# Keys, queries, values and weights laid out by the launcher as the kernel reads them, in a sliding-window attention with two feed-forward layers

## The chip, the cores and the metric

The kernel runs on one core of one Trainium2 chip. The metric is the device time of one execution in microseconds, the median of several runs. The core's engines run side by side and wait for one another through semaphores: TensorE (PE in the profile; PEld is its weight load), VectorE (DVE), ScalarE (ACT), GpSimd (POOL) and SyncE (SP), which only issues transfers here. Each engine works off its own instructions in the order in which they were queued. Work done by the launcher on the host is not part of the time.

## The reference

Attention over 2 batches of 8 heads, 768 positions, head dimension 64. A position sees the first `n_sink` positions (4) and the last `window` positions (128). Its output, heads side by side, runs through two feed-forward layers over 1536 tokens of width 512.

```python
scores = (q @ k.T) / sqrt(64)                      # per batch and head
keep = (pos_k < n_sink) | (0 <= pos_q - pos_k < window)
a = softmax(where(keep, scores, -1e9))
x = (a @ v)                                        # -> [1536, 512]
x = ((x @ w_a) * (x @ w_b)) @ w_out                # 512 -> 1536 -> 512
h = maximum(x @ w_in2, 0)
out = (h * h) @ w_out2                             # 512 -> 2048 -> 512
```

The weights arrive as 64-bit floats, q, k and v as 32-bit floats.

## The kernel before, in words

**Groups and steps.** A group is one block of 128 queries of 4 heads; there are 24, numbered batch, then block `i` (0 to 5), then half of the heads `m`. `attention_fast` runs 27 steps. In step g it goes through the list ORDER (L28), which names pieces of work with a lag: `("scores", 0)` is the scores of group g, `("rec", -1)` the reciprocal of the sums of group g - 1, `("x", -3)` the values of group g - 3. The lists are a schedule by hand: TensorE, VectorE, ScalarE and GpSimd take their instructions in the order in which they are emitted (L800). SP's transfers are not in that list and follow the emission as their buffers come free.

**One group's way.** Two steps ahead transfers bring k and q with tokens in the partitions (L179), one step ahead v (L193). One step ahead TensorE transposes keys and queries (`pt`, L233, four transposes), ScalarE copies them out of PSUM (`kq`, L239) into a buffer of slots, and for block 0 GpSimd copies the first 8 keys behind each slot as sink keys (L241). In its own step: scores (L258; for a block i > 0 against the block itself, the block before it, and the sink keys), then on VectorE a predicated copy that merges the two triangles (L271) and the masked maximum (L274), then on ScalarE four exponentials with their sums (L282). One step later: reciprocal (L287, the first VectorE instruction of a step), the scaled sink columns (L305), normalizing on VectorE (L292) and ScalarE (L297), TensorE's transposes of probabilities (L312, L336). Two steps later ScalarE copies (L316) and GpSimd cuts the two triangles (L327, L329). Three steps later the values (L355) and the sink values (L360), and the split of the result into a high and a low part (L368, L371).

**Sink values.** `vs` holds the values of the first 8 positions of each head, arranged and zero-padded so that one matmul adds them for a pair of heads; it is needed from step 5 on (group 2). `sink_load` clears a buffer on GpSimd and issues 24 transfers on SP, emitted in front of step 1; `sink_split` makes the parts on ScalarE (L216) and VectorE (L217), emitted behind step 2.

**Masks.** `setup` and `masks` build three masks on VectorE from `n_sink` and `window`, which come as single values and are spread over the partitions by a matmul (L106). `flag` tests whether the fast way applies; otherwise `attention_any` would run, which it does not with these inputs.

**Beside the attention.** The weights' 64-bit floats are decoded in pieces of 128 x 512 (`Weights.stages`): ScalarE L552, VectorE L556, L557, L560 in one step, VectorE L563, ScalarE L568, VectorE L570 in the next. DECODE (L33) lists the steps in which a piece is begun. From step 10 on each step also holds one fill of 12 matmuls of the first feed-forward layer (L660). From step 9 on (WIDE) the attention has two PSUM buffers fewer, which go to the fills. `warm` issues dummy matmuls: 14 at the beginning (WARM0), 4 and 3 in steps 0 and 1 (WARM1). Behind the 27 steps follow the remaining fills and the rest of both layers (`Ffn.block`, L660 and L701), with the other weights decoded on the way. `Weights.load` brings one piece per transfer into one of three raw buffers (L537).

Of the kernel before, what the change touches and what calls it, by code (L numbers as in the profile page):

```python
# [61 lines left out]
def setup(tc, cp, tp, n_sink, window):  # L62
    nc = tc.nc
    c = Attn()
    ident = tp.tile([P, P], F32, name="ident")
# [1 line left out]
    c.identr = cp.tile([P, P], F32R, name="identr")
    nc.vector.tensor_copy(c.identr, ident)
    c.ident = c.identr.bitcast(F32)

    raw = cp.tile([1, 4], I32, name="raw")
    nc.scalar.dma_start(raw[:, 0:2], n_sink.bitcast(I32).partition_broadcast(1))
    nc.scalar.dma_start(raw[:, 2:4], window.bitcast(I32).partition_broadcast(1))
# [17 lines left out]
    c.rel0 = tp.tile([P, P], F32, name="rel0")  # L91
    v.scalar_tensor_tensor(out=c.rel0, in0=c.upf, scalar=BIG, in1=d, op0=ALU.mult, op1=ALU.add)
    lo = cp.tile([1, 2], F32, name="lo_f")
    hi = cp.tile([1, 2], F32, name="hi_f")
# [2 lines left out]
    c.par0 = cp.tile([1, 2], F32, name="par0")
    v.scalar_tensor_tensor(out=c.par0, in0=hi, scalar=4294967296.0, in1=lo, op0=ALU.mult, op1=ALU.add)
    return c


def masks(tc, cp, tp, c, ps):

    nc = tc.nc
    v = nc.vector
    nc.tensor.matmul(ps, lhsT=c.one, rhs=c.par0, start=True, stop=True)  # L106
# [754 lines left out]
```

## Time and profile before

| | |
|---|---|
| median of 3 runs | 676.22 us (676.17 to 676.25) |
| profiled execution | 678.09 us |
| its span, first to last instruction | 676.40 us |
| mean granted TensorE clock | 0.986 |
| TensorE busy | 652.0 us (96%) |
| VectorE busy | 401.7 us (59%) |
| ScalarE busy | 290.7 us (43%) |
| GpSimd busy | 30.2 us (4%) |

The page gives busy time of each engine and its tenths in 40 slices of the span. [...] The timeline lists instructions with start and length; a bracket behind a row says how long the engine was idle before it and what ended the wait. The chain of waits follows the work that ended last back to the start.

### The profile page before, as it was taken

The numbers are of one execution on the slowest core, as the hardware profiler recorded it, in microseconds if no ns is written. First come the engines' busy times: TensorE is split into PE (matmuls) and PEld (weight loads), VectorE is DVE, ScalarE is ACT, GpSimd is POOL, SyncE is SP. The second block draws the span as 40 slices with busy tenths as digits, with TensorE's granted clock in tenths as the row PEclk, the third lists the DMA queues.
The fourth block names the chain that finished last, engine by engine and source line by source line (L and its number), as shares of the span: only waits on it lengthen the run. The fifth ranks groups of instructions, "written<-read, shape, count | busy, mean of one in ns | idle before, by whom it ended". The sixth has DMA issues, their size and how long they took to land.

```text
span 676.4 us, 8976 instructions
## 1 busy us (share of the span) xinstructions
PE 652.0 (96%) x3267; PEld 528.6 (78%) x3267; DVE 401.7 (59%) x950; ACT 290.7 (43%) x676; POOL 30.2 (4%) x53
## 2 busy tenths in 40 slices
PE   7578999999999999999999999999999999999996
PEld 5356877778788888888888888888888888888884
DVE  5698986762689872588641789535824232333323
ACT  6676886761444532545321446324532222222221
POOL 1131202120000000000000000000000000000000
PEclk9697999999999999999999999999999999999999
DMA  5853543310164550045400043200200000001011
GB/s 136 197 121 85 145 123 85 85 33 0 63 188 133 165 169 1 32 150 162 155 1 0 32 125 125 94 0 32 63 0 1 0 1 0 1 1 62 23 40 68
DMA packets 65560, 48.99 MB, mean 72 GB/s; under 512 B 39908, under 2 KB 60388, under 8 KB 65508
## 3 DMA queue, kind: packets, MB, share of 16 engines
q1 hardware_dynamic: 65504, 48.34, 24.8%
q8 instruction: 27, 0.44, 0.3%
q14 instruction: 25, 0.20, 0.1%
q10 hardware_dynamic: 4, 0.00, 0.0%
HBM read 45.19 MB, written 3.15 MB: 71 GB/s over the span
## 4 chain that ended last, share of the span: by engine, by line
PE 92%; DVE 4%; ACT 1%; DMA 1%; SPq 1%; issue 0%; DVEq 0%; ACTq 0%
PE psa L660 48%; PE acc L701 34%; PE x L355 3%; PE sc L258 3%; PE pt L233 1%; PE ptp L312 1%; ACT ex L282 1%; PE x L360 1%; DMA qraw<-in_q_dram 1%; SPq L211 1%; DVE ex L274 1%; DVE ex L292 1%; DVE sc L271 1%; PE psw L380 1%; DVE xl L371 0%
## 5 line engine op out<-in xcount | busy, mean ns | idle before, releaser
L660 PE MATMUL psa<-xh,wh 128*128 128x512 f32 x480 | 188.9, 393 | 0.8 <-DVE gs L677 0.8
L660 PE MATMUL psa<-xh,wl 128*128 128x512 f32 x480 | 187.0, 390 | 0.0
L660 PE MATMUL psa<-xl,wh 128*128 128x512 f32 x480 | 186.8, 389 | 0.0
L660 PEld LDWEIGHTS psa<-xh,wh 128*128 128x128 f32 x480 | 90.4, 188 | 19.8 <-DVE gs L677 1.3
L660 PEld LDWEIGHTS psa<-xh,wl 128*128 128x128 f32 x480 | 90.1, 188 | 19.0
L660 PEld LDWEIGHTS psa<-xl,wh 128*128 128x128 f32 x480 | 90.3, 188 | 18.3
L740 DVE TENSOR_TENSOR g<-u 128x512 f32<-128x512 f32 x48 | 33.1, 690 | 111.2 <-ACT u L730 111.2
L730 ACT ACTIVATE u<-psa 128x512 f32<-128x512 f32 x48 | 28.7, 598 | 119.0 <-PE psa L660 119.0
L701 PE MATMUL acc<-wh,gl 128*128 128x512 f32 x192 | 74.7, 389 | 0.0
L701 PE MATMUL acc<-wl,gh 128*128 128x512 f32 x192 | 74.7, 389 | 0.0
L58 ACT CAST gh<-g 128x512 fp32r<-128x512 f32 x72 | 44.6, 620 | 64.7 <-DVE g L740 34.8
L552 ACT ACTIVATE wtmp<-wraw 128x512 f32<-128x512 f32 x68 | 45.5, 672 | 54.0 <-DMA wraw<-in_moe_w_in_dram 17.9
L59 DVE TENSOR_TENSOR gl<-g,gh 128x512 fp32r<-128x512 f32 x72 | 49.6, 689 | 31.2 <-ACT gh L58 30.9
L701 PE MATMUL acc<-wh,gh 128*128 128x512 f32 x192 | 62.7, 389 | 0.0
L568 ACT CAST wh<-wtmp 128x512 fp32r<-128x512 f32 x68 | 41.8, 618 | 35.5 <-DVE wtmp L563 15.5
L570 DVE TENSOR_TENSOR wl<-wtmp,wh 128x512 fp32r<-128x512 f32 x68 | 46.5, 685 | 17.0 <-ACT wh L568 15.9
L701 PE MATMUL acc<-gl,wh 128*128 128x512 f32 x144 | 56.0, 389 | 0.0
L701 PE MATMUL acc<-gh,wl 128*128 128x512 f32 x144 | 55.9, 389 | 0.0
L560 DVE SCALAR_TENSOR_TENSOR wtmp<-wraw,wtmp 128x512 int32<-128x512 int32 x68 | 47.4, 699 | 0.6
L701 PE MATMUL acc<-gh,wh 128*128 128x512 f32 x144 | 47.3, 389 | 0.0
L563 DVE SCALAR_TENSOR_TENSOR wtmp<-wraw,wtmp 128x512 int32<-128x512 int32 x68 | 46.5, 684 | 0.2
L701 PEld LDWEIGHTS acc<-wl,gh 128*128 128x128 f32 x192 | 36.1, 188 | 7.5
(92 smaller groups left out, 753.4 us busy)
## 6 DMA issues: line engine op xcount, KB each, us to landing
wraw<-in_moe_w_out_dram SPq DMA_DIRECT2D x28, 512.0 KB
wraw<-in_moe_w_in_dram SPq DMA_DIRECT2D x16, 512.0 KB
wraw<-in_moe_w_a_dram SPq DMA_DIRECT2D x12, 512.0 KB
wraw<-in_moe_w_b_dram SPq DMA_DIRECT2D x12, 512.0 KB
vraw<-in_v_dram SPq DMA_DIRECT2D x24, 128.0 KB
out_dram<-part SPq DMA_DIRECT2D x12, 256.0 KB
kraw<-in_k_dram SPq DMA_DIRECT2D x23, 128.0 KB
qraw<-in_q_dram SPq DMA_DIRECT2D x23, 128.0 KB
```

Of the source, the lines that this page charges most:

```text
L58: nc.scalar.copy(hi, src)
L59: (lo_eng or nc.vector).tensor_sub(lo, src, hi.bitcast(F32))
L258: nc.tensor.matmul(o, lhsT=half(flat, r)[:, qp, 0:P], rhs=y, start=True, stop=True)
L552: a = nc.scalar.activation(tf, up.bitcast(F32), AF.Abs)
L560: nc.vector.scalar_tensor_tensor(out=t, in0=up, scalar=0x3FFFFFFF, in1=t, op0=ALU.bitwise_or, op1=ALU.bitwise_and)
L563: nc.vector.scalar_tensor_tensor(out=t, in0=low, scalar=29, in1=t, op0=ALU.logical_shift_right, op1=ALU.bitwise_or)
L568: nc.scalar.copy(hi, tf)
L570: nc.vector.tensor_sub(lo, tf, hi.bitcast(F32))
L660: self.tc.nc.tensor.matmul(ps, lhsT=w[:, kt, :], rhs=x[:, kt, ts], start=n == 0, stop=n == 3 * KT - 1)
L701: mm = nc.tensor.matmul(acc[d], lhsT=a, rhs=b_, start=f == 0 and j == 0, stop=f == NF - 1 and j == 2)
L730: nc.scalar.activation(u, pa, AF.Relu)
L740: nc.vector.tensor_mul(g, u, u)
```

## The change

The launcher gets a function `layout`, and the kernel takes its inputs as laid out there:

- q and k with two heads' dimensions in the 128 partitions, per block of 128 positions; k with the 8 sink keys behind each block. So scores read them as they come, and `transposes`, `transposes_copy` and GpSimd's copy are gone, with `pt` and `kq` in ORDER. A slot of keys and a tile of queries now hold a whole block (8 heads), loaded every second step.
- v per block with all heads, one transfer for two groups.
- `vs` comes ready with its zeros, one transfer a batch; the two splits are emitted behind steps 3 and 6 (VS).
- `n_sink` and `window` come spread over 128 partitions in one transfer; the spreading matmul is gone. Only mask 0 is built ahead of step 0; masks 1 and 2 and the flags are emitted behind it.
- weight pieces are contiguous; w_a, w_b and w_in2 rows are 4 KB in a partition instead of four runs of 1 KB.
- the dummy matmuls of WARM1 are gone; DECODE begins a piece in step 8 and none in step 22.

```diff
-    ("rec", -1), ("x", -3), ("th", -2), ("sp", -1), ("norm", -1), ("scores", 0), ("pt", 1), ("xh", -3),
-    ("normA", -1), ("xl", -3), ("fm", 0), ("soft0", 0), ("fu", 0), ("stt2", -1), ("soft1", 0), ("abs", 0),
-    ("pst", -1), ("kq", 1), ("st", -1), ("fill", 0), ("exp0", 0), ("sts", -1), ("ts", 0), ("cast", -1), ("stt",
-    0), ("lu", -2), ("lo", -1), ("exp1", 0), ("ptp", -1)]
-DECODE = [2, 6, 9, 10, 11, 12, 13, 15, 18, 20, 22]
+    ("rec", -1), ("x", -3), ("th", -2), ("sp", -1), ("norm", -1), ("scores", 0), ("xh", -3), ("normA", -1),
+    ("xl", -3), ("fm", 0), ("soft0", 0), ("fu", 0), ("stt2", -1), ("soft1", 0), ("abs", 0), ("pst", -1), ("st",
+    -1), ("fill", 0), ("exp0", 0), ("sts", -1), ("ts", 0), ("cast", -1), ("stt", 0), ("lu", -2), ("lo", -1),
+    ("exp1", 0), ("ptp", -1)]
+DECODE = [2, 6, 8, 9, 10, 11, 12, 13, 15, 18, 20]
 WIDE = 9
-SINK = (1, 2)
+VS = (3, 6)
 PINNED = 3
 WARM0 = 14
-WARM1 = {0: 4, 1: 3}
-NV, NEX, NTH, NLU, NSP = 8, 3, 2, 2, 2
+NQ, NV, NEX, NTH, NLU, NSP = 3, 5, 3, 2, 2, 2
+NK = 4
...
+    raw = cp.tile([P, 4], I32, name="raw")
+    nc.scalar.dma_start(raw, span.bitcast(I32))
...
+def later_masks(tc, cp, tp, c):
+    v = tc.nc.vector
+    m0, m1, m2 = c.m
+    c.up = cp.tile([P, P], I32, name="upi")
+    v.tensor_copy(c.up, c.upf)
+
+    out_of(v, m2[:, 0:P], c.rel, c.w)
+    v.tensor_copy(m2[:, P:SW], c.sink[:, 0:SK])
 
...
+    keys = p1.tile([P, NK, H // 2, SW], F32, name="keys")
+    queries, vals = {}, {}
...
+    def load_kq(n, part=slice(0, H // 2)):
+        if n >= B * NB:
             return
...
+        if n not in queries:
+            queries[n] = p2.tile([P, H // 2, P], F32, name="queries", tag="queries", bufs=NQ)
+        b, i = divmod(n, NB)
+        nc.sync.dma_start(keys[:, n % NK, part], k[b, i, :, part])
+        nc.sync.dma_start(queries[n][:, part], q[b, i, :, part])
+
+    def load_v(n):
+        if n >= B * NB:
+            return
+        vals[n] = p2.tile([P, H, D], F32, name="values", tag="values", bufs=NV)
+        nc.sync.dma_start(vals[n], v[n // NB, n % NB])
+
+    with tc.high_priority(offset=1000):
+        load_kq(0, slice(0, 2))
+        load_kq(0, slice(2, 4))
+    load_kq(1)
+    load_v(0)
 
...
-    def sink_load():
-        nc.gpsimd.memset(vsr, 0.0)
-        for kind in range(3):
-            for j in range(GH):
-                for b in range(B):
-                    p0 = (kind * GH + j) * SK
-                    nc.sync.dma_start(vsr[p0:p0 + SK, b, j // 2:H // 2:2, (j % 2) * D:(j % 2 + 1) * D],
-                                      v[b, j:H:GH, 0:SK, :].rearrange("m s d -> s m d"))
-
-    def sink_split():
-        for b in range(B):
-            nc.scalar.copy(vs[:, b], vsr[:, b])
-            nc.vector.tensor_sub(vs[64:96, b], vsr[64:96, b], vs[64:96, b].bitcast(F32))
-
...
+    def sink_load(b):
+        vsr[b] = p1.tile([96, H // 2, P], F32, name="vsr", tag="vsr")
+        nc.sync.dma_start(vsr[b], vs_in[:, b])
+
+    def sink_split(b):
+        nc.scalar.copy(vs[:, b], vsr[b])
+        nc.vector.tensor_sub(vs[64:96, b], vsr[b][64:96], vs[64:96, b].bitcast(F32))
...
-        pt = pts[g] = bank("pt").rearrange("p (j a) t -> p j a t", j=2)
-        for j, t in enumerate((kr, qr)):
-            for pp in range(2):
-                nc.tensor.transpose(pt[:, j, pp], t[:, 2 * pp:2 * pp + 2, :].rearrange("t h d -> t (h d)"), c.ident)
-        vals[g] = vr
-
-    def transposes_copy(g):
-        b, i, m = groups[g]
-        ks, qs = (i % 2) * 2 + m, 4 + g % 2
-        nc.scalar.copy(kq[:, ks:qs + 1:qs - ks, :, 0:P], pts.pop(g))
-        if i == 0:
-            nc.gpsimd.tensor_copy(kq[:, m:m + 3:2, :, P:SW],
-                                  kq[:, ks, :, 0:SK].unsqueeze(1).to_broadcast([P, 2, 2, SK]))
...
         for pp, sc in enumerate(scs[g]):
...
-                    y = half(flat, r)[:, kp:kp + 5:4]
+                    (u0, u1), _ = around(g)
+                    y = half(keys, r)[:, u0:u1 + 1:u1 - u0, 2 * m + pp]
...
     warm(WARM0)
-    transposes(0)
-    masks(tc, cp, tp, c, bank("par")[:, 0, 0:2])
-    transposes_copy(0)
     for g in range(N + 3):
         if g == WIDE:
             banks.pop()
             wide.close()
             beside.open()
-        if g == SINK[0]:
-            sink_load()
-        load(g + 2)
+        if g % 2 == 0:
+            load_kq(g // 2 + 2)
+            load_v(g // 2 + 1)
+        if g == 0:
+            sink_load(0)
         beside.fetch(g)
-        if g in WARM1:
-            warm(WARM1[g])
         for name, lag in ORDER:
             if name in stages:
                 if 0 <= g + lag < N:
                     stages[name](g + lag)
             else:
                 beside.stage(name, g + lag)
-        if g == SINK[1]:
+        if g == 0:
+            later_masks(tc, cp, tp, c)
             flag(tc, cp, c)
-            sink_split()
+        if g in VS:
+            sink_split(VS.index(g))
+            if g == VS[0]:
+                sink_load(1)
...
-        def cols(w, f):
-            return w.bitcast(I32).rearrange("(k p) f -> p k f", p=P)[:, :, 2 * f * P:2 * (f + 1) * P]
-
-        def rows(w, f):
-            return w.bitcast(I32)[f * P:(f + 1) * P, :].unsqueeze(1)
+        FF1, FF2 = w_a.shape[0], w_in2.shape[0]
+
+        def piece(w, f):
+            return w.bitcast(I32)[f]
...
+def layout(inputs):
+
+    import numpy as np
+
+    def pairs(a, n):
+
+        B, H, S, D = a.shape
+        a = a.reshape(B, H // 2, 2, S // n, n, D).transpose(0, 3, 2, 5, 1, 4)
+        return a.reshape(B, S // n, 2 * D, H // 2, n)
+
+    def blocks(w, inner):
+
+        if inner:
+            K, FF = w.shape
+            w = w.reshape(K // P, P, FF // P, P).transpose(2, 1, 0, 3)
+        return np.ascontiguousarray(w.reshape(-1, P, 512)).view(np.int64)
+
+    q, k, v = (np.asarray(inputs[n]) for n in "qkv")
+    B, H, S, D = v.shape
+    out = {"q": pairs(q, P)}
+    sinks = pairs(k[:, :, 0:SK], SK)
+    out["k"] = np.concatenate([pairs(k, P), np.broadcast_to(sinks, (B, S // P, *sinks.shape[2:]))], axis=4)
+    out["v"] = v.reshape(B, H, S // P, P, D).transpose(0, 2, 3, 1, 4)
+
+    vs = np.zeros((3, 4, SK, B, H // 4, 2, 2, D), v.dtype)
+    for j in range(4):
+        vs[:, j, :, :, :, j // 2, j % 2] = v[:, j::4, 0:SK].transpose(2, 0, 1, 3)
+    out["vs"] = vs.reshape(12 * SK, B, H // 2, 2 * D)
+    out["span"] = np.broadcast_to(np.stack([inputs["n_sink"], inputs["window"]]).astype(np.int64), (P, 2))
+    for n in _INS[5:]:
+        out[n] = blocks(np.asarray(inputs[n]), not n.endswith("out"))
+    return out
```

## Rows read from the trace of the kernel before

**Rows 1.** The page's busy tenths of TensorE in 40 slices of the span.

```profile
PE   7578999999999999999999999999999999999996
```

**Rows 2.** Windows, us from:to, length, busy us (instructions) per engine, clock, transfers.

```profile
57.34:63.31 5.97, 5.97 (x32) 4.58 (x33) 5.65 (x16) 2.41 (x8) 1.67 (x2) 0.50 0.11 25
63.31:99.14 35.83, 35.83 (x261) 28.13 (x261) 32.11 (x110) 28.62 (x95) 6.04 (x10) 1.00 0.53 140
99.14:137.65 38.51, 38.51 (x284) 30.08 (x283) 28.79 (x111) 27.92 (x94) 7.79 (x12) 1.00 0.32 83
```

**Rows 3.** Timeline of the start: start us, length us, engine, line, what.

```profile
1.07 3.17 PE L380 MATMUL psw<-zero 128*128 128x256 bf16 x14 [1.07 <-DVE zero L787]
...
2.76 0.16 DVE L95 CAST lo_f<-raw 1x2 f32<-1x2 uint32 x1 [0.41 <-DMA raw<-in_window_dram]
...
6.14 0.72 PE L258 MATMUL sc<-kq 64*128 64x128 f32 x8
...
7.55 0.28 DVE L274 CUSTOM_DVE_ANT_0 ex<-sc,m 128x128 f32<-128x128 f32 x1
```

**Rows 4.** Timeline around 9 to 23 us: SP's queue and VectorE.

```profile
9.45 10.79 SPq L211 DMA_DIRECT2D wraw<-in_v_dram  x24
...
16.35 0.69 DVE L560 SCALAR_TENSOR_TENSOR wtmp<-wraw,wtmp 128x512 int32<-128x512 int32 x1
...
21.83 1.28 DVE L217 TENSOR_TENSOR vs<-wraw,vs 32x512 fp32r<-32x512 f32 x2 [4.22 <-ACT vs L216]
```

**Rows 5.** Timeline of VectorE, first instruction of steps 3, 5, 6, 7, 8, 10.

```profile
23.14 0.17 DVE L287 TENSOR_SCALAR ss<-ss 128x4 f32<-128x4 f32 x1
...
32.64 0.17 DVE L287 TENSOR_SCALAR ss<-ss 128x4 f32<-128x4 f32 x1 [0.42 <-ACT ex L282]
...
37.09 0.17 DVE L287 TENSOR_SCALAR ss<-ss 128x4 f32<-128x4 f32 x1 [0.42 <-ACT ex L282]
...
43.13 0.60 DVE L287 TENSOR_SCALAR ss<-ss 128x4 f32<-128x4 f32 x1
...
48.38 0.16 DVE L287 TENSOR_SCALAR ss<-ss 128x4 f32<-128x4 f32 x1
...
59.22 0.59 DVE L287 TENSOR_SCALAR ss<-ss 128x4 f32<-128x4 f32 x1
```

**Rows 6.** Windows, one microsecond while keys, queries and values are loaded.

```profile
25.00:26.00 1.00, 1.00 (x8) 0.68 (x8) 1.00 (x6) 0.80 (x4) 0.00 (x0) 0.50 1.41 229
```

**Rows 7.** Chain of waits, a step of the wide stage: start us, length us, what.

```profile
99.14 2.77 PE psa L660 x12
...
104.86 0.59 PE pt L233 x4
...
105.56 2.77 PE psa L660 x12
```

**Rows 8.** Timeline of ScalarE, first decode of a weight piece.

```profile
13.95 0.66 ACT L552 ACTIVATE wtmp<-wraw 128x512 f32<-128x512 f32 x1
```

**Rows 9.** Timeline of VectorE, a late decode instruction and the next one.

```profile
45.84 0.69 DVE L563 SCALAR_TENSOR_TENSOR wtmp<-wraw,wtmp 128x512 int32<-128x512 int32 x1
46.44 0.42 DVE L271 COPY_PREDICATED sc<-upi,sc 128x256 f32<-128x256 int32 x1
```

**Rows 10.** Timeline of VectorE, waits in the wide stage.

```profile
68.48 0.42 DVE L371 TENSOR_TENSOR xl<-x,xh 128x256 fp32r<-128x256 f32 x1 [1.11 <-ACT xh L368]
...
104.19 0.42 DVE L371 TENSOR_TENSOR xl<-x,xh 128x256 fp32r<-128x256 f32 x1 [1.03 <-ACT xh L368]
```

**Rows 11.** Chain of waits, scores of a group in steps 10 and 11.

```profile
59.94 2.12 PE sc L258 x8
...
68.04 1.12 PE sc L258 x8
```

More of the change, by code (lines that the diff above doesn't have):

```diff
@@ L59, in split, with setup @@
     (lo_eng or nc.vector).tensor_sub(lo, src, hi.bitcast(F32))
-def setup(tc, cp, tp, n_sink, window):
+def setup(tc, cp, tp, span):
     nc = tc.nc
     c = Attn()
+    raw = cp.tile([P, 4], I32, name="raw")
+    nc.scalar.dma_start(raw, span.bitcast(I32))
     ident = tp.tile([P, P], F32, name="ident")
     make_identity(nc, ident)
[L67 to L73, printed above, removed]
     warm = tp.tile([P, 1], F32, name="warm")
-    nc.scalar.activation(warm, c.ident[:, 0:1], AF.Exp)
+    nc.scalar.activation(warm, ident[:, 0:1], AF.Exp)
     v = nc.vector
-    c.one = cp.tile([1, P], F32, name="one")
-    v.memset(c.one, 1.0)
     d = tp.tile([P, P], F32, name="d")
@@ L85, in setup @@
     v.tensor_scalar(out=c.upf, in0=d, scalar1=0.0, scalar2=None, op0=ALU.is_lt)
-    c.up = cp.tile([P, P], I32, name="upi")
-    v.tensor_copy(c.up, c.upf)
     c.rel = tp.tile([P, P], F32, name="rel")
     v.scalar_tensor_tensor(out=c.rel, in0=c.upf, scalar=float(P), in1=d, op0=ALU.mult, op1=ALU.add)
[L91 to L94, printed above, removed]
+    rel0 = tp.tile([P, P], F32, name="rel0")
+    v.scalar_tensor_tensor(out=rel0, in0=c.upf, scalar=BIG, in1=d, op0=ALU.mult, op1=ALU.add)
+    lo = cp.tile([P, 2], F32, name="lo_f")
+    hi = cp.tile([P, 2], F32, name="hi_f")
     v.tensor_copy(lo, raw.bitcast(U32)[:, 0:4:2])
     v.tensor_copy(hi, raw[:, 1:4:2])
[L97 to L106, printed above, removed]
     par = cp.tile([P, 2], F32, name="par")
-    v.tensor_copy(par, ps)
+    v.scalar_tensor_tensor(out=par, in0=hi, scalar=4294967296.0, in1=lo, op0=ALU.mult, op1=ALU.add)
     c.ns = par[:, 0:1]
@@ L257, in scores @@
                     o = sc[:, r, 0:2 * SW].rearrange("q (u s) -> q u s", u=2)
-                nc.tensor.matmul(o, lhsT=half(flat, r)[:, qp, 0:P], rhs=y, start=True, stop=True)
+                nc.tensor.matmul(o, lhsT=half(queries[n], r)[:, 2 * m + pp], rhs=y, start=True, stop=True)
     def maxima(g, pp):
@@ L292, in normalize, with normalize_a @@
         nc.vector.tensor_mul(ex[:, 0:2, 0:P], ex[:, 0:2, 0:P], ss[:, 0:2].unsqueeze(2).to_broadcast([P, 2, P]))
-    def normalize_too(g):
+    def normalize_a(g):
         ex, ss = pns[g][0:2]
-        for h in range(2, GH):
+        for h in range(2, 4):
             nc.scalar.mul(ex[:, h, 0:P], ex[:, h, 0:P], ss[:, h:h + 1])
@@ L354, in values @@
             for h in range(GH):
-                nc.tensor.matmul(half(x, h % 2)[:, h // 2], lhsT=vals[g - 2 * j][:, h], rhs=probs_t[:, h],
+                nc.tensor.matmul(half(x, h % 2)[:, h // 2], lhsT=vals[g // 2 - j][:, GH * m + h], rhs=probs_t[:, h],
                                  start=j == 0 and h < 2, stop=False, skip_group_check=True)
@@ L384, in attention_fast @@
                   soft1=lambda g: maxima(g, 1), exp0=lambda g: exps(g, 0), exp1=lambda g: exps(g, 1), rec=reciprocal,
-                  norm=normalize, normA=normalize_too, sp=sinks, pst=sinks_turn, st=sinks_copy, sts=sinks_low, pt=transposes, kq=transposes_copy,
-                  x=values, xh=x_high, xl=x_low)
+                  sp=sinks, pst=sinks_turn, st=sinks_copy, x=values, xh=x_high, xl=x_low,
+                  norm=normalize, normA=normalize_a, sts=sinks_low)
     warm(WARM0)
-    transposes(0)
-    masks(tc, cp, tp, c, bank("par")[:, 0, 0:2])
-    transposes_copy(0)
     for g in range(N + 3):
@@ L770, in sliding_window_moe_kernel @@
 @with_exitstack
-def sliding_window_moe_kernel(ctx, tc, q, k, v, n_sink, window, w_a, w_b, w_out, w_in2, w_out2, out):
+def sliding_window_moe_kernel(ctx, tc, q, k, v, vs, span, w_a, w_b, w_out, w_in2, w_out2, out):
     nc = tc.nc
     NT, DM = out.shape
-    B, H, S, D = q.shape
     cp = ctx.enter_context(tc.tile_pool(name="cp", bufs=1))
@@ L789, in sliding_window_moe_kernel @@
     tp = mk.enter_context(tc.tile_pool(name="mk", bufs=1, side="right"))
-    c = setup(tc, cp, tp, n_sink, window)
+    c = setup(tc, cp, tp, span)
     def run(attend):
@@ L849 @@
     from concourse.bass_utils import run_bass_kernel_spmd as _run
+    inputs = layout(inputs)
     arrays, shapes = {}, {}
```

120 lines of the change are left out of this document (42 added, 78 removed).

## The prediction

> **What bounds the kernel now.** I read the page first, for the busy tenths in 40 slices, then the windows by stage, the chain of waits, and last the timeline of one engine at a time. TensorE is full from about 57 us to the end [rows 1, 2]: the feed-forward part behind the attention is a back-to-back stream of matmuls, and nothing in the diff takes a matmul out of it. The weights reach it in another layout only; no wait of TensorE for a weight transfer stands in that stretch, so I cost that edit at 0 there, and its cover is the decode that runs ahead (three raw buffers). What can change lies in the first 144 us, and there are four stretches with four different bounds.
>
> First the start. Fourteen dummy matmuls end at 4.24 us, then TensorE transposes group 0, ScalarE copies, and the scores of group 0 start at 6.14; their maxima wait on until 7.55, because VectorE builds all three masks first from numbers that came at 2.76 [rows 3].
>
> Second the stall. The zero-padded sink values come in 24 transfers of 4 KB, and issuing them keeps SP's queue for 10.8 us. The split of these values stands in VectorE's order ahead of step 3, so VectorE ends its last decode instruction of step 2 at 17.04 and takes up step 3 at 23.14 [rows 4, 5]. [...]
>
> Third the narrow stage, steps 3 to 9, where no feed-forward work fills in. One step is read from one reciprocal of the sums (L287, first VectorE instruction of a step) to the next: 4.45 us for a step without a decode of weights, 6.04 and 5.25 for the two steps that share the decode begun in step 6 [rows 5]. In the 4.45 VectorE is idle 0.42, waiting for the last exponential of ScalarE; TensorE has room. So this stage is bound by VectorE and, between maxima and the next reciprocal, by ScalarE's exponentials; the transposes and their copy are off that path.
>
> Fourth the wide stage, step 10 on, with twelve fill matmuls a step. TensorE is busy 35.83 of 35.83 us in steps 10 to 15, but VectorE is 32.11 busy there, since nearly every step decodes weights; in steps 16 to 21 it is 28.79 of 38.51 [rows 2]. There TensorE alone sets the pace, 6.42 us a step, of which four transposes are 0.59 [rows 7].
>
> **The change part by part.** All terms are against the profiled execution (678.09 us, of that 676.40 span; the median of the runs is 676.22, so 1.87 us below). I carry the difference over unchanged.
>
> Start: keys and queries come with the head dimension in the partitions, so scores(0) can begin where the dummies end, 4.24 instead of 6.14: 1.9 us. The maxima now need only mask 0 (made inside the setup from a transfer that has 128 partitions instead of one; I take its landing as near the 2.76 of before), so they can start half a set of scores (0.5) after 4.24, up to 7.55 - 4.75 = 2.8 us earlier. The other two masks and the flags are put behind step 0 in VectorE's order, ahead of the next reciprocal, and eat part of it. I take 2.3; bounds 1.9 and 2.8. [rows 3]
>
> Stall: 23.14 - 17.04 = 6.1 us [rows 4, 5] go, as SP issues two transfers for the sinks instead of 24, the first in step 0 and needed in step 3. What is late next is the first piece of weights. SP issues it behind eleven transfers, 2.9 MB with itself. The absolute value of that piece (L552) stands in ScalarE's order ahead of the exponentials of step 2, at 13.95 before [rows 8] and so at 11.7 now; whatever it waits, the exponentials, and VectorE's next reciprocal behind them, wait too. At the 229 GB/s of a stretch full of 256-byte rows [rows 6], 2.9 MB from about 2 us land at 14.5, which is 2.8 late; the new rows are 1 to 4 KB, so the rate should be better and the lower bound is 0. I take 0.7, nearer to 0. [...]
>
> So step 3 starts 2.3 + 6.1 - 0.7 = 7.7 us earlier.
>
> Narrow stage, losses. The two splits of sink values stood in the stall and now stand behind steps 3 and 6. VectorE's part is 1.28 us for two [rows 4], and it waits for a ScalarE copy that is queued behind that step's exponentials; behind it in VectorE's order is the next reciprocal. Both steps carry a decode, so VectorE has no idle time left to give: 1.4 for both, bounds 0.6 (one of them hidden) and 2.5 (the copy exposed as well). The decode of step 22 is moved to step 8. In step 22 it is free, since TensorE bounds there; in step 8 it falls on VectorE. Alone it would cost (6.04 - 4.45) + (5.25 - 4.45) = 2.4 [rows 5]; but step 9 already begins a decode, so the two late instructions of the one from step 8 come in whole, 0.60 each from start to start [rows 9]. Steps 8 and 9 took 10.84, 0.35 more than 4.45 + 6.04 [rows 5], and a little of that may be used up: 1.5 + 1.2 = 2.7, bounds 1.2 and 2.9. The copy of transposed keys and queries (ScalarE) and POOL's copy of sink keys save nothing here, since ScalarE waits for VectorE's maxima ahead of the exponentials. Loads of keys, queries and values go out every second step, two steps further ahead; SP's one new wait (second sink transfer, for the buffer that the first split frees in step 3) has the loads of step 4 behind it, which are used in step 8: nothing. Sum of the stage: -4.1. Step 10 then starts 7.7 - 4.1 = 3.6 us earlier.
>
> Wide stage, steps 10 to 15: six times 0.59 = 3.5 us leave TensorE, but VectorE's idle time is all that can be won, at most 35.83 - 32.11 = 3.7 and surely only the longer waits, such as the 1.11 us in which it waits for TensorE's values by way of ScalarE [rows 2, 10]. I take 2.4, the middle of 1.1 and 3.7.
>
> Wide stage, steps 16 to 21: 38.51 us for six steps, TensorE-bound, VectorE with waits of 1.03 us a step [rows 2, 10]. 6 x 0.59 = 3.5 [rows 7], all on the path; this is the upper bound too, and the lower is 2.4, if the two decode steps (18 and 20) gain nothing.
>
> Clock: the seven dummy matmuls of steps 0 and 1 (WARM1) and the 44 transposes ahead of step 10 are gone, so TensorE is idle more in the narrow stage. At 0.50 a set of scores takes 2.12 instead of 1.12 [rows 11]. A wide step without its fill (2.77) and transposes (0.59) is 6.42 - 2.77 - 0.59 = 3.06 [rows 7], which is also a narrow step's TensorE work now: at full clock 1.4 us of the 4.45 are room, at the low clock 6.1 are needed and a step without decode loses 1.7. Steps with a decode take about that long anyway. I take 0.3 for a short low spell, bounds 0 and 4.5 (below).
>
> Sum: 3.6 + 2.4 + 3.5 - 0.3 = 9.2 us; 678.09 - 9.2 = 668.9 for a profiled execution and 676.2 - 9.2 = 667.0 for the median.
>
> **The rivals.** (a) VectorE bounds the wide stage further than I think, or the narrow stage loses to the low clock: of the bad ends (splits 2.5, first weights 2, clock 3, wide stage 1.1 and 2.4) two or more together leave 2 to 6 us, 670 to 674. For it: VectorE is 90% busy in steps 10 to 15 [rows 2]; against it: it has room from step 16. (b) The moved work hides: the splits and the decode at step 8 cost 0.6 and 1.2, the start gives 2.8, the weights are not late, the wide stage gives 3.7: 14 us, 662. For it: some instructions on VectorE took longer at places that will shift, as the reciprocal's first at 43.13 with 0.60 against 0.17 [rows 5]; against it: the 0.42 idle of a step. (c) The change does not do what it says: step 3 waits for something else that also came near 21 us, and the 6.1 stay. Then 9.2 - 6.1 = 3.1 us are left, 673; with the losses of (a) beside it, no change. Against it: the split on VectorE waited 4.22 us with nothing between [rows 4], and the loads that SP had queued behind the 24 transfers move forward with them.
>
> (d) Slower, by one mechanism, the clock. [...] A narrow step then needs twice the TensorE work: 6.1 us as above [rows 7, 11], against 4.45 to 7 for VectorE, some 4.5 us over the stage (1.7 in steps 4 and 5, 0.9 in step 7, little in the others); that alone leaves a gain. It decides from the point at which the low clock lasts into the wide stage: there a step is 2 x 5.83 = 11.7, so 5.8 us lost each, and two such steps turn the 9.2 into -7: 683. Against it: after 57 to 63 us at 0.50 the engine, which worked without gaps, was back at 1.00 [rows 2], and a low-clock step has no gaps. [...]
>
> **How the numbers follow.** Forecast, 664.5 to 669.5: 0.54. (a) 0.20, (b) 0.15, (c) 0.05, of it 0.04 with the losses that make it no change, (d) 0.06. The range takes in most of (a) and (b): 662.5 to 671.5. A measurement of this kernel tells 0.2%, 1.35 us, from no change. Faster 0.90, same 0.04, slower 0.06.
>
> **What would show it.** Right: no gap on VectorE or TensorE near 17 to 24 us; the first maxima near 4.8; the reciprocal of step 3 near 15.4 and that of step 10 near 55.6; steps 8 and 9 together near 13.5 us; from step 16 on 5.83 us between fills. Wrong: a wait of ScalarE for the first weights over 2 us, several windows at 0.50 before step 10, a pace in steps 16 to 21 that stays at 6.4, or VectorE waiting for ScalarE's copy of sink values behind steps 3 and 6.

## The result, and the profile of the kernel after

| | before | after |
|---|---|---|
| median | 676.24 us (676.17 to 676.35) | 669.75 us (669.68 to 669.98) |
| after / before | | 0.9905 [0.9887, 0.9922] |
| profiled execution | 678.09 | 669.81 |
| its span | 676.4 | 668.1 |
| VectorE busy | 401.7 | 405.7 |
| TensorE busy | 652.0 | 643.5 |

The change makes the kernel 6.5 us faster by the medians and 8.3 us by the two profiled executions; forecast were 9.2 on either, 667.0 us, with a range of 662.5 to 671.5. By the interval of the ratio the gain is 5.3 to 7.6 us, so the 9.2 are outside it. The sign, the places and most of the sizes held. The 2.7 us that are missing have two sources, and each is a step of the sum: 1.8 lie in the difference between a profiled execution and the median, which I carried over unchanged, and 0.9 in the sum itself.

The page of the kernel after: busy tenths and granted clock in 40 slices, and its transfers.

```profile
PE   7878999999999999999999999999999999999996
DVE  6899998834798942799441889426924232333323
PEclk9777999999999999999999999999999999999998
DMA packets 17410, 49.46 MB, mean 74 GB/s; under 512 B 2064, under 2 KB 2576, under 8 KB 17360
```

TensorE is still full from the fifth slice (67 us) on, as in [rows 1]: behind that, time can be won only by work that TensorE no longer has, the transposes. VectorE stands at 8 or 9 tenths from the second slice to the eighth. Packets fell from 65560 to 17410, those under 512 B from 39908 to 2064.

Timeline of the start of the kernel after, and ScalarE's first decode of weights (columns as in [rows 3]).

```profile
3.21 0.17 DVE L86 CAST lo_f<-raw 128x2 f32<-128x2 uint32 x1 [0.99 <-DMA raw<-in_span_dram]
4.16 1.23 PE L225 MATMUL sc<-keys,queries 64*128 64x128 f32 x8
5.01 0.29 DVE L241 CUSTOM_DVE_ANT_0 ex<-sc,m 128x128 f32<-128x128 f32 x1 [0.52 <-PE sc L225]
...
12.88 0.67 ACT L509 ACTIVATE wtmp<-wraw 128x512 f32<-128x512 f32 x1 [1.47 <-DMA wraw<-in_moe_w_a_dram]
```

Scores start at 4.16 instead of 6.14, the maxima at 5.01 instead of 7.55 [rows 3]. The spread parameters landed 0.45 later than the single values had, without effect, since the maxima wait for TensorE. ScalarE now waits 1.47 us for the first piece of weights.

Timeline of VectorE in the kernel after: first instruction (L254) of steps 3 to 10, the two splits (L200), and the decode (L517, L527) ahead of a step.

```profile
15.15 0.17 DVE L254 TENSOR_SCALAR ss<-ss 128x4 f32<-128x4 f32 x1
...
20.15 0.68 DVE L200 TENSOR_TENSOR vs<-vsr,vs 32x512 fp32r<-32x512 f32 x1 [0.21 <-ACT vs L199]
20.86 0.49 DVE L254 TENSOR_SCALAR ss<-ss 128x4 f32<-128x4 f32 x1
...
25.36 0.17 DVE L254 TENSOR_SCALAR ss<-ss 128x4 f32<-128x4 f32 x1 [0.42 <-ACT ex L249]
...
30.17 0.17 DVE L254 TENSOR_SCALAR ss<-ss 128x4 f32<-128x4 f32 x1 [0.80 <-ACT ex L249]
...
35.84 1.02 DVE L200 TENSOR_TENSOR vs<-vsr,vs 32x512 fp32r<-32x512 f32 x1
36.87 0.51 DVE L254 TENSOR_SCALAR ss<-ss 128x4 f32<-128x4 f32 x1
...
42.04 0.16 DVE L254 TENSOR_SCALAR ss<-ss 128x4 f32<-128x4 f32 x1
...
47.35 1.17 DVE L517 SCALAR_TENSOR_TENSOR wtmp<-wraw,wtmp 128x512 int32<-128x512 int32 x1
48.44 0.60 DVE L254 TENSOR_SCALAR ss<-ss 128x4 f32<-128x4 f32 x1
...
54.01 1.15 DVE L517 SCALAR_TENSOR_TENSOR wtmp<-wraw,wtmp 128x512 int32<-128x512 int32 x1
55.08 1.11 DVE L527 TENSOR_TENSOR wl<-wtmp,wh 128x512 fp32r<-128x512 f32 x1
56.12 0.16 DVE L254 TENSOR_SCALAR ss<-ss 128x4 f32<-128x4 f32 x1
```

Step 3 starts 8.0 us earlier than in [rows 5] (23.14), step 10 only 3.1 earlier (59.22): 4.9 us are given back in between. Steps 8 and 9 take 14.08 us together. Several rows show instructions at well over their usual length: L517 at 1.17 and 1.15 (0.69 elsewhere), L527 at 1.11 (0.69), the split at 1.02 after one of 0.68, and L254 at 0.49 to 0.60 instead of 0.17.

Windows of the kernel after (columns as in [rows 2]); the last one is steps 8 and 9.

```profile
45.00:57.00 12.00, 10.02 (x56) 7.29 (x57) 11.48 (x36) 7.61 (x27) 3.35 (x4) 0.50 0.32 103
42.04:56.12 14.08, 10.47 (x56) 7.47 (x58) 13.50 (x41) 8.98 (x31) 4.59 (x6) 0.55 0.35 118
```

VectorE (third busy figure) is busy 96% in both. TensorE was granted 0.50 of its full clock from 45 to 57 us and is still busy only 10.02 of 12 there. Taken in half microseconds, its clock is 0.50 from 22.9 to 29.7 us and from 43.4 to 57.0 us, and 1.00 elsewhere up to 75 us.

Chain of waits of the kernel after, from the fill of step 16 to that of step 18 (what is left out repeats the pattern).

```profile
93.38 2.76 PE psa L617 x12
96.14 0.44 PE ptp L279 x4
96.58 1.00 issue
97.58 1.09 PE x L322 x16
...
99.05 1.12 PE sc L225 x8
...
100.41 2.75 PE psa L617 x12
...
106.11 0.24 PE pst L303
106.36 2.76 PE psa L617 x12
```

A step of the wide stage is now 5.95 us (100.41 to 106.36) against 6.42 [rows 7]. The transposes `pt` are gone, but `pst`, which stood behind them with 0.11 us, takes 0.24 behind the scores: 0.47 a step are won, not 0.59. And in step 17 TensorE stands still for 1.00 us, which the step before the change did not have.

### The profile page after: what moved, and what is told of

Same layout as the page of the kernel before. It is cut to its first block, busy times and chain, and to the rows that moved or that the text cites. A ratio compares the mean times of both kernels' runs of the same rounds, so it can differ in the third digit from the quotient of the medians.

```text
span 668.1 us, 8625 instructions
## 1 busy us (share of the span) xinstructions
PE 643.5 (96%) x3162; PEld 520.6 (78%) x3162; DVE 405.7 (61%) x948; ACT 280.9 (42%) x652; POOL 29.7 (4%) x48
## 2 busy tenths in 40 slices
DMA packets 17410, 49.46 MB, mean 74 GB/s; under 512 B 2064, under 2 KB 2576, under 8 KB 17360
## 4 chain that ended last, share of the span: by engine, by line
PE 89%; DVE 7%; ACT 1%; DMA 1%; SPq 1%; issue 1%; DVEq 0%
PE psa L617 48%; PE acc L658 34%; PE x L322 2%; PE sc L225 2%; DMA wraw<-in_moe_w_a_dram 1%; PE ptp L279 1%; DVE ex L241 1%; PE x L327 1%; DVE wtmp L517 1%; ACT ex L249 1%; DVE sc L238 1%; DVE wl L527 1%; PE pst L303 1%; DVE ex L259 0%; DVE wtmp L520 0%
## 5 line engine op out<-in xcount | busy, mean ns | idle before, releaser
L527 DVE TENSOR_TENSOR wl<-wtmp,wh 128x512 fp32r<-128x512 f32 x68 | 48.3, 712 | 16.4 <-ACT wh L525 15.2
L517 DVE SCALAR_TENSOR_TENSOR wtmp<-wraw,wtmp 128x512 int32<-128x512 int32 x68 | 47.9, 707 | 0.6
L520 DVE SCALAR_TENSOR_TENSOR wtmp<-wraw,wtmp 128x512 int32<-128x512 int32 x68 | 46.5, 685 | 0.2
L249 ACT ACTIVATE ex<-ex,nb 128x136 f32<-128x136 f32 (+1 forms) x96 | 38.2, 400 | 13.5 <-DVE nb L241 12.9
```

The source lines that it names most:

```text
L249: nc.scalar.activation(ex[:, h, 0:w], ex[:, h, 0:w], AF.Exp, bias=nb[:, h:h + 1], scale=-1.0, accum_out=ss[:, h:h + 1])
L517: nc.vector.scalar_tensor_tensor(out=t, in0=up, scalar=0x3FFFFFFF, in1=t, op0=ALU.bitwise_or, op1=ALU.bitwise_and)
L520: nc.vector.scalar_tensor_tensor(out=t, in0=low, scalar=29, in1=t, op0=ALU.logical_shift_right, op1=ALU.bitwise_or)
L527: nc.vector.tensor_sub(lo, tf, hi.bitcast(F32))
```

## The experiments

The kernel after was timed in one set of four executions, its variants in other sets, in which the kernel before had medians of 675.75 to 676.75 us. So a difference of under about 1 us between a variant and after tells nothing by itself.

**The kernel before once more.** No edit. The question was whether the profiled execution of before, 1.87 us above its median, was typical.

> The kernel before, unchanged, for a second profile. The profiled execution of before took 678.09 us, 1.87 above its median, and that of the changed kernel 669.81, as its median; the prediction carried the 1.87 over. Theory 1 (that one profiled execution was slow by chance, most likely in the low-clock spell at 57 to 63 us): this profile has a span nearer to 674.5, and step 10 starts earlier than 59.2. Rival (profiling always costs this kernel that much): span near 676.4 again, with the same spell.

Measured: 676.34 us (676.12 to 677.93), ratio 0.9998 [0.9985, 1.0011]; the profiled execution took 677.92 us with a span of 676.0, again high, and its clock is 0.50 from 56.1 to 63.0 us, as it was from 56.7 to 63.5 in the first. That is nearer to the rival than to theory 1. But four of the 22 executions beside it that were not profiled took 677.9 us or more too, and all lie between 675.3 and 678.5 us. So an execution need not be profiled to be that long; whether profiling makes it likelier for this kernel, two profiles don't tell. The profiled execution of after (669.81) sits on its median (669.75). Steps read from one profile against the other add up to the 8.3 us between the profiles; 1.8 of these are not in the medians.

**The stall alone.** The kernel before, with nothing changed but the sink values, zero-padded by the launcher:

```diff
     def sink_load():
-        nc.gpsimd.memset(vsr, 0.0)
-        for kind in range(3): ...            # 24 transfers
+        for bb in range(B):
+            nc.sync.dma_start(vsr[:, bb], vs_in[:, bb])
```

> The kernel before with one part of the change alone: the sink values come zero-padded from the launcher in two transfers at the same place of the order, everything else as before. The prediction's term for the stall is 6.1 us. Theory 1: 670.1 us, step 3 starts near 17 instead of 23.1. Rival (c) of the prediction (step 3 waits for something else that also comes late): 673 us or more.

Timeline of VectorE in that kernel: the two splits, then the first instruction of steps 3 and 10 (line numbers are five lower than in [rows 4] and [rows 5]).

```profile
17.93 1.28 DVE L212 TENSOR_TENSOR vs<-wraw,vs 32x512 fp32r<-32x512 f32 x2
19.24 0.17 DVE L282 TENSOR_SCALAR ss<-ss 128x4 f32<-128x4 f32 x1
...
55.63 0.16 DVE L282 TENSOR_SCALAR ss<-ss 128x4 f32<-128x4 f32 x1
```

Chain of waits of that kernel, the fill of step 16.

```profile
94.20 2.78 PE psa L655 x12
```

Measured: 673.73 us (672.42 to 675.78), ratio 0.9959 [0.9937, 0.998]. Step 3 starts 3.9 us earlier: the 4.22 us of waiting in [rows 4] are gone, and the flags and splits still stand ahead of step 3. By its time alone the run lies on the rival's side (673 or more); the trace decides against it, since nothing is waited for between the last decode and step 3. So the mechanism is the predicted one. My 6.1 held about 2 us of VectorE's own work, flags and splits. The change moves the flags behind step 0 and the splits behind steps 3 and 6; the sum charged both there, so it came out right.

This trace shows one thing more. Its execution (673.38 us) is near its median, and its clock is 0.50 from 46.7 to 53.5 us, ahead of the fills, where the two profiles of the kernel before have their low spell at some 56 to 63, over step 10. From the start of step 10 to the fill of step 16 it takes 38.57 us (55.63 to 94.20); the two profiles of before take 39.92 (59.22 to 99.14, [rows 5, 7]) and 39.94. From the fill of step 12 on all three agree (23.3), so the 1.3 us lie in steps 10 and 11: TensorE worked there without a gap at 0.50 in before [rows 2]. That low spell may be most of what lies between the profiled execution of before and its median; no profile of one of its shorter executions is there to show it.

**The first weights first.** In the kernel after, the first piece of weights is issued ahead of the loads of step 0:

```diff
+        if g == 0:
+            beside.W.load()
         if g % 2 == 0:
             load_kq(g // 2 + 2)
...
-        beside.fetch(g)
+        if g != 1:
+            beside.fetch(g)
```

> The changed kernel with the load of the first weight piece issued ahead of the keys and queries of block 2 (in step 0) instead of in step 1. In the profile ScalarE waited 1.47 us for this piece. Theory 1: the wait is gone and step 3 starts near 14 instead of 15.15; 668.5 us. Rival (the keys and values that now come later are missed instead, or the gain is lost again before step 16, where VectorE is saturated): 669.5 us or more.

Measured: 669.48 us (668.32 to 669.68), ratio 0.989 [0.9874, 0.9906], the same as after. ScalarE no longer waits (its first decode stands at 11.32), step 3 starts at 14.33, 0.8 earlier, and the fill of step 26 is still 0.74 earlier. The time is the rival's nevertheless (669.5 or more). What lies behind, to the end of the span, takes 519.1 us here and 518.5 in after (519.3 in before): the gain is within what the rest scatters. A second thing came out beside: with these transfers untouched, ScalarE's first decode stood at 12.49 to 14.10 us in the profiles of after and its variants (waits of 0.71 to 2.69). The predicted 0.7 (0 to 2.8) had its size from the right bounds, but it is a scatter, not a number.

**The decode of step 8 back in step 22.**

```diff
-DECODE = [2, 6, 8, 9, 10, 11, 12, 13, 15, 18, 20]
+DECODE = [2, 6, 9, 10, 11, 12, 13, 15, 18, 20, 22]
```

> The changed kernel with the list of decode steps of before (a piece begun in step 22, none in step 8). Theory 1 (VectorE bounds steps 3 to 16, the moved piece costs what the prediction priced, 2.7 us): 667.0 us, steps 8 and 9 together near 11 us instead of 14.1. [...]

Measured: 667.71 us (667.23 to 668.09), ratio 0.987 [0.9847, 0.9892]; steps 8 and 9 take 10.86 us instead of 14.08. Beginning that piece in step 8 costs 2.0 us by the medians and 2.4 by the profiles, near the 2.7 of the prediction, and buys nothing. Step 3 started 0.6 later here, since ScalarE waited 2.06 us for the first weights, so the price by itself is rather more.

**The splits elsewhere.** Behind steps 4 and 14, which begin no decode, instead of 3 and 6.

```diff
-VS = (3, 6)
+VS = (4, 14)
```

> The changed kernel with the two splits of sink values behind steps 4 and 14 instead of 3 and 6. Theory 1 (in steps 3 and 6, which carry a decode, the split stands on the path with ScalarE's copy in front of it, 1.2 and 1.5 us by the chain; step 14 has a little room): 668 to 669 us. Rival (VectorE has no room anywhere before step 16, so the cost only moves): within 0.5 us of 669.75.

Measured: 672.19 us (670.48 to 672.98), ratio 0.9926 [0.9899, 0.9954]: all four executions above those of after, though the intervals of the two ratios overlap, and neither expectation met. In step 4 the split waits 0.93 us for ScalarE's copy and the step takes 6.02 instead of 4.50; step 14 takes 6.11 instead of 4.90, and its split waits 0.64. The idle 0.42 of such a step [rows 5] is no room for a piece of 0.68 with its wait. Of the loss of 2.4 us, 1.2 stand ahead of step 3 and belong to the first weights, which in this profile kept ScalarE waiting 2.69.

**The clock.** Dummy matmuls in steps 0 to 9 of the kernel after.

```diff
+WARM1 = {0: 4, 1: 3, 2: 4, 3: 8, 4: 4, 5: 4, 6: 8, 7: 4, 8: 8, 9: 4}
...
         beside.fetch(g)
+        if g in WARM1:
+            warm(WARM1[g])
```

> The changed kernel with dummy matmuls at the head of steps 0 to 9 (4, 3, 4, 8, 4, 4, 8, 4, 8, 4), so that TensorE's gaps in the narrow stage are filled. Clock theory: no window at 0.50 before step 10, and steps 4 to 6 and 8 to 10 faster, 668 us or less. VectorE theory: the clock is kept but the time is within 0.7 us of 669.75, or up to 1 us longer where dummies delay scores.

Windows of that kernel, then its VectorE timeline at the start of steps 5, 6, 8, 9 and 10 (L255 there).

```profile
21.00:30.00 9.00, 7.12 (x68) 5.32 (x70) 7.75 (x33) 6.16 (x25) 2.44 (x4) 1.00 0.26 87
...
42.00:51.00 9.00, 6.29 (x52) 4.28 (x50) 8.62 (x29) 5.83 (x20) 2.91 (x4) 1.00 0.32 111
51.50:60.00 8.50, 7.09 (x33) 5.26 (x34) 8.13 (x28) 5.65 (x21) 1.67 (x2) 0.50 0.31 98
```

```profile
25.45 0.17 DVE L255 TENSOR_SCALAR ss<-ss 128x4 f32<-128x4 f32 x1 [0.42 <-ACT ex L250]
...
29.89 0.17 DVE L255 TENSOR_SCALAR ss<-ss 128x4 f32<-128x4 f32 x1 [0.43 <-ACT ex L250]
...
41.75 0.16 DVE L255 TENSOR_SCALAR ss<-ss 128x4 f32<-128x4 f32 x1
...
48.15 0.59 DVE L255 TENSOR_SCALAR ss<-ss 128x4 f32<-128x4 f32 x1
...
55.83 0.16 DVE L255 TENSOR_SCALAR ss<-ss 128x4 f32<-128x4 f32 x1
```

Measured: 670.69 us (669.51 to 671.54), ratio 0.9915 [0.9888, 0.9941], no faster than after. The dummies did not remove the low clock, they moved it: here it is 0.50 from 37.7 to 41.2 us and from 51.4 to 61.6, which takes in most of step 10 and its fill, the first; that fill takes 4.50 us instead of some 2.8. So neither theory's condition came about, and the time alone says little. Single steps say more. Step 8 takes 6.40 us here at 1.00, and 6.40 in after, where the clock was 0.50 for the last 5.1 us of it: VectorE sets this pace (6.12 us busy of the 6.40 in after), and the low clock cost nothing in this step. Step 5, which begins no decode, takes 4.44 here at 1.00 and 4.81 in after at 0.50: there ScalarE waits 1.53 us for TensorE's `pst`, its exponentials end later, and VectorE waits 0.80 for them instead of 0.43. So the low clock cost after 0.4 us in step 5.

**The transposes back.** Four transposes of an identity a step, behind the scores, into a `pt` tile of the same PSUM buffers, read by nobody: TensorE's work alone, without the copy and the waits. The edit in ORDER is left out here.

```diff
+    def turned(g):
+        pt = bank("pt")
+        for j in range(GH):
+            nc.tensor.transpose(pt[:, j], c.ident, c.ident)
```

> The changed kernel with four TensorE transposes a step put back where those of keys and queries stood (of the identity, never read; no copy behind them). Theory 1 (they cost only in the steps in which TensorE sets the pace, from step 16 on 0.47 us a step as the two chains show, and nothing where VectorE is saturated): 671.5 to 673 us. Rival (they cost 0.59 in all thirteen wide steps): 677 us. Clock: if transposes keep the clock up, the low spell at 44 to 57 us is gone.

Chain of waits of that kernel, one step of the wide stage.

```profile
101.77 2.77 PE psa L623 x12
...
107.49 0.59 PE pt L231 x4
108.08 0.11 PE pst L309
108.19 2.77 PE psa L623 x12
```

Measured: 674.23 us (672.75 to 676.11), ratio 0.9972 [0.9956, 0.9988]. The step is 6.42 again, with `pst` back at 0.11, so the transposes' net price is 0.47 in these steps. To the fill of step 26 the profile loses 3.65 us against after: 1.56 in steps 12 to 15 (0.4 a step), and 1.65 in the six steps behind, since the 1.00 wait of step 17 is gone with them (that step takes 6.40). The price of the transposes lay between the two expectations. The page's clock digits are 9668 in the first four slices, no better than the 9777 of after: put back, the transposes do not hold the clock up.

**The held-up instructions: GpSimd's cuts.** The long rows above have a partner. Timeline of GpSimd in the kernel after, the cuts of step 8.

```profile
47.34 0.64 POOL L294 TENSOR_SCALAR_AFFINE_SELECT lu<-th 128x512 f32<-128x512 f32 x1 [3.78 <-ACT th L283]
47.93 1.08 POOL L296 TENSOR_SCALAR_AFFINE_SELECT lu<-th 128x512 f32<-128x512 f32 x1
```

VectorE's L517 starts at 47.35, just behind the first cut, and takes 1.17 instead of 0.69; the second cut takes 1.08 instead of 0.64; VectorE's L254 at 48.44 takes 0.60 instead of 0.17 and ends with it. By these lengths the two engines take turns. VectorE's instructions that read PSUM keep their length beside a cut (L338 and L238 0.42 us beside the cuts of step 5 at 26.49; L241 0.30 beside those that the second edit below puts there). Four that were held up have two inputs in SBUF: L517, L527 (1.11 at 55.08), L259 (0.85 instead of 0.42 at 25.95) and L200 (1.02 at 35.84, instead of 0.68). L254 has only one input, 128x4, and is held up too (0.60); the reciprocal behind it kept its 0.18 us beside a cut at 21.39.

Two edits test it. The first leaves the cuts out, and part of the computation with them; the copies of probabilities, which the values then read themselves, get four buffers instead of two:

```diff
-NQ, NV, NEX, NTH, NLU, NSP = 3, 5, 3, 2, 2, 2
+NQ, NV, NEX, NTH, NLU, NSP = 3, 5, 3, 4, 2, 2
...
-        nc.gpsimd.affine_select(...)         # both cuts
+        lus[g] = (ths[g], ths[g])
```

> The changed kernel without GpSimd's cuts of the two triangles (the values are then multiplied by uncut probabilities; part of the computation is left out). Theory 1 (VectorE instructions that work from SBUF alone are held up while GpSimd cuts: 0.60 instead of 0.17, 0.85 instead of 0.42, 1.17 instead of 0.69, 1.12 instead of 0.69, about 0.9 us a step in steps 5 to 13): 663 to 666 us. Rival (VectorE is bound by its own work, the long instructions only look long because they wait for ScalarE): within 1 us of 669.75.

The second moves ScalarE's copy, which releases the cuts, behind ScalarE's part of normalizing, so that the cuts start later in a step:

```diff
-    ("rec", -1), ("x", -3), ("th", -2), ("sp", -1), ("norm", -1), ("scores", 0), ("xh", -3), ("normA", -1),
+    ("rec", -1), ("x", -3), ("sp", -1), ("norm", -1), ("scores", 0), ("xh", -3), ("normA", -1), ("th", -2),
```

> The changed kernel with ScalarE's copy of transposed probabilities put behind its normalizing instead of at the head of a step, so that GpSimd's cuts run beside the maxima (which read PSUM) instead of beside reciprocal, normalizing and the last decode instruction. Theory 1: the long VectorE instructions are shorter, 667 to 669 us. Rival (the collision only moves, or the later cut delays the values): 669.5 us or more.

VectorE's instructions grouped by line, 17 to 100 us (busy us, mean ns of one | idle before): the kernel after, then without cuts (L522 and L512 are after's L527 and L517), then with the cuts later.

```profile
L259 DVE TENSOR_TENSOR ex<-ex,ss 128x256 f32<-128x256 f32 x14 | 8.0, 573 | 0.1
L527 DVE TENSOR_TENSOR wl<-wtmp,wh 128x512 fp32r<-128x512 f32 x9 | 7.9, 880 | 0.1
L517 DVE SCALAR_TENSOR_TENSOR wtmp<-wraw,wtmp 128x512 int32<-128x512 int32 x8 | 6.9, 868 | 0.3
L520 DVE SCALAR_TENSOR_TENSOR wtmp<-wraw,wtmp 128x512 int32<-128x512 int32 x9 | 6.2, 688 | 0.0
```

```profile
L259 DVE TENSOR_TENSOR ex<-ex,ss 128x256 f32<-128x256 f32 x15 | 6.3, 419 | 0.1
L522 DVE TENSOR_TENSOR wl<-wtmp,wh 128x512 fp32r<-128x512 f32 x9 | 6.2, 688 | 0.1
...
L512 DVE SCALAR_TENSOR_TENSOR wtmp<-wraw,wtmp 128x512 int32<-128x512 int32 x8 | 5.5, 692 | 0.3
```

```profile
L520 DVE SCALAR_TENSOR_TENSOR wtmp<-wraw,wtmp 128x512 int32<-128x512 int32 x9 | 7.7, 860 | 0.0
L259 DVE TENSOR_TENSOR ex<-ex,ss 128x256 f32<-128x256 f32 x15 | 6.3, 419 | 0.1
L527 DVE TENSOR_TENSOR wl<-wtmp,wh 128x512 fp32r<-128x512 f32 x9 | 6.2, 687 | 0.1
...
L517 DVE SCALAR_TENSOR_TENSOR wtmp<-wraw,wtmp 128x512 int32<-128x512 int32 x8 | 5.5, 692 | 0.3
```

Without cuts: 663.71 us (662.21 to 665.17), ratio 0.9804 [0.9772, 0.9836], 6.0 us under after; VectorE's busy time falls by 9.7 us to 396.0. The 6.0 are all that the cuts cost the kernel after: the collisions, and with them whatever the values lose by waiting for the cuts, which this run doesn't tell apart. With the cuts later: 667.10 us (666.11 to 668.43), ratio 0.9858 [0.9829, 0.9887], 2.6 under after. L527, L517 and L259 have their plain length; part of the loss moved to L520 in the middle of a step.

**The same move in the kernel before.** Is the collision the change's doing?

```diff
-    ("rec", -1), ("x", -3), ("th", -2), ("sp", -1), ("norm", -1), ("scores", 0), ("pt", 1), ("xh", -3),
-    ("normA", -1), ("xl", -3), ...
+    ("rec", -1), ("x", -3), ("sp", -1), ("norm", -1), ("scores", 0), ("pt", 1), ("xh", -3),
+    ("normA", -1), ("th", -2), ("xl", -3), ...
```

> The kernel before with the copy of transposed probabilities behind the normalizing, nothing else. Theory 1 (GpSimd's cuts hold VectorE up in the kernel before as well, but there the steps from 10 on are paced by TensorE, so less is lost by it): 674 to 675.5 us, a smaller gain than the 2.6 us that the same edit gave the changed kernel. Rival (the collision is as dear there): 673.5 us or less.

Measured: 674.27 us (673.98 to 674.61), ratio 0.9964 [0.9951, 0.9977], 2.0 under the kernel before of the same chip (676.27). So the collision was there before, as the 0.60 and 0.59 in [rows 5] had shown, and the move ends it (that instruction's mean falls from 251 to 166 ns, that of L560 from 825 to 693); the 2.6 that the move brings in after are little more, and these runs don't tell the two apart. New in after is that L527 meets a cut (880 ns on the mean; its counterpart in before, L570, had 687).

**Together.** The cuts later and the decode back in step 22, both edits as above.

> The changed kernel with both edits that helped: the copy of transposed probabilities behind the normalizing, and the decode steps of before. Theory 1 (both take time from VectorE in steps 3 to 16, where it is saturated, so they add): 665 us. Rival (they overlap, since less VectorE work in steps 8 to 10 leaves fewer collisions there): 666.5 us or more.

Measured: 663.78 us (662.07 to 664.89), ratio 0.9809 [0.979, 0.9827], 6.0 under after, where the two gains by themselves (2.6 and 2.0) give 4.7; with executions from 662.07 to 664.89 us that is not told apart from a plain sum. Step 10 starts at 50.47 and step 11 at 56.82, near the place of after's step 10. With the first weights first as well:

> The same with the first weight piece loaded in step 0 as well. Theory 1: 663.5 to 664 us. Rival: no better than without.

Measured: 663.47 us (663.05 to 664.24), ratio 0.9809 [0.9796, 0.9823]: no more than the two. Both versions beat the kernels before and after, by 1.9% and some 0.9%.

## Why the prediction was right, and where it was off

Steps of the sum against the two profiled executions:

| step | predicted | measured |
|---|---|---|
| step 3 starts earlier (start, stall, first weights) | 7.7 | 8.0 |
| narrow stage, splits | -1.4 | -1.7 |
| narrow stage, decode in step 8 | -2.7 | -3.2 |
| narrow stage, steps 4 and 7 | 0 | 0.4 |
| low clock | -0.3 | -0.4 (step 5) |
| wide stage, steps 10 to 15 | 2.4 | 2.7 |
| wide stage, steps 16 to 21 | 3.5 | 1.7 |
| behind step 21 | 0 | 0.8 |
| sum | 9.2 | 8.3 |
| profile to median | 0 | -1.8 |
| median | 9.2 | 6.5 |

The start, the stall and its replacement by a wait for weights went as written: step 2 starts 2.6 us earlier (I took 2.3 for the start), and from there to step 3 another 5.4 are won (6.1 - 0.7); maxima at 5.01 (forecast 4.8), step 3 at 15.15 (15.4), step 10 at 56.12 (55.6). That the wait for the first weights came so near its 0.7 is luck, as its scatter shows. The rate was better than the 229 GB/s of [rows 6]: 299 GB/s on the mean from 2 to 12 us of the kernel after (237 from 2 to 4, 354 from 8 to 10); no run changed the length of the rows alone.

The narrow losses had the right mechanism. The splits are read from steps 3 and 6: 5.71 and 6.70 us against 4.70 and 6.04, together 1.7. The decode is steps 8 and 9: 14.08 against 10.84, 3.2, where I said 2.7. I took the two late instructions at 0.60 each; L527 took 1.11 in step 9, because it met a cut. In the medians the undone move is worth 2.0, which is inside the bounds 1.2 to 2.9. Step 4 won 0.3 and step 7 0.1 that no term held.

The 2.7 of steps 10 to 15 came near their 2.4 for another reason than I gave. I let VectorE bound them and counted its idle time. But from 71.4 us on, at the fill of step 12, the chain of waits runs on TensorE, and from that fill to the one of step 16 it takes 21.71 us against 23.33: 1.6 won, four times the 0.4 that the transposes cost there when they were put back. The other 1.0 lies in steps 10 and 11, where the kernel before had TensorE at 0.50 (some 1.3 us, by the run with the sinks alone) and after had it back at 1.00 from 57.0 us on. My clock term asked only what the low clock would cost the kernel after; what it already cost the profiled execution of before stood in no term. That the two made 2.7 is luck.

The mis-sized term is the wide stage from step 16. I called 6 x 0.59 = 3.5 "all on the path" and named 2.4 the least. Measured are 1.7, from fill to fill (36.80 us for six steps against 38.51). Two pieces fail. First, the price of the transposes: 0.47 net, since `pst` costs 0.24 behind scores and 0.11 behind transposes; that is 2.8 for six steps. Second, the 1.00 of step 17. The trace names no releaser for it. By the code the values take the PSUM buffer that `pst` of the step before had (two buffers, in turn), whose last reader is VectorE's L314; VectorE gets to that at 97.19, for 0.28, and TensorE starts at 97.58. Up to there VectorE ran behind, from the decode steps 8 to 15. The step is 7.03 us in after and 7.04 with the decode in step 22, but 6.14 with the cuts later and 5.93 without cuts, which speaks for VectorE as the cause; no run changed the buffers, so it isn't shown. It is rival (a)'s mechanism, VectorE binding further than I took it, but with one wait instead of a pace.

The 0.8 behind step 21 lie behind the fill of step 26 (519.3 us in before, 518.5 in after); no run shows a cause, and variants scatter as much. Without them the sum would have been 1.7 too large and not 0.9.

The last step that failed is a sentence I thought harmless: the difference between the profile and the median "carried over unchanged". After does not have it. Both profiled executions of before were 1.6 to 1.9 us above their medians, and both had the low spell over step 10. That fits the clocks of the 46 executions of before beside the experiments: all of 677 us or more were granted 0.988 or less on the mean, and all with 0.989 or more took less than 676.3. So the spell is the likeliest cause of most of the 1.8, and the 1.0 won in steps 10 and 11 would then be a part of it; it isn't shown.

Rival (b) is out: splits and decode did not hide. Rival (c) is out by the trace of the sink values alone. Rival (d) did not come: the granted clock was 0.50 from 43.4 to 57.0 us and 1.00 behind that, at the first fills. It is nearer than that sounds: with the dummies, with the splits moved and with the weights first, the low spell lasted until 60.6 to 61.6 us, into the first fill. The clock term had the right size, and the wrong price beneath it: step 5, without a decode and at 0.50 for 4.4 of its 4.8 us, lost 0.4 and not 1.7.

Of the signs that I named for "wrong", two appeared: VectorE waited for ScalarE's copy of sink values, 0.21 us behind step 3 and nothing behind step 6, and there are windows at 0.50 ahead of step 10, which cost little, because VectorE was full beside most of them. Fills are 5.95 us apart instead of the 5.83 named for "right", and steps 8 and 9 take 14.08 instead of 13.5.

## What to carry to other kernels

A step that one engine bounds pays for every instruction that is moved into it (steps 8 and 9 took 3.2 us more), and pays again for what the new neighbours hold up: ask of each moved instruction what runs beside it on the other engines (L527, beside a cut of GpSimd, took 1.11 us instead of 0.69). When work is taken out of a chain, price what is left by its length behind its new predecessor, not by its row in the old chain (`pst` took 0.24, not 0.11). And before a profiled execution stands for the median, run the old kernel more often, and look where its low-clock spells lie: here its single executions differed by 3 us, more than the 1.8 that the prediction lost by it.
